# Two sliding-window and two linear-attention layers with their backward pass: from layer-by-layer stages to fused streams of token tiles

## The chip, the cores and the metric

The kernel runs on one core of a Trainium2 chip. The metric is device time in microseconds (us) of one execution; medians of a few executions are quoted. Engines are named as in the profile: PE (matrix products), PEld (its weight loads), DVE (here the multiplies and sums on whole tiles), ACT (here exp and copies), POOL (here the masks), and SP, which here issues DMA. A profile also gives the granted clock of PE as a share of full speed.

## The reference

Four residual layers on 2,048 tokens of 640 features, 32 heads of 20: linear attention (A), causal sliding-window attention of 256 tokens (B), A, B, each behind a layer norm. A and B each have one set of weights that two layers share. The outputs are the result and the gradients of the input and of the four weights.

```python
def _A_ref(x, wqkv, wo):            # q, k, v per head
    phi = lambda t: jnp.where(t > 0, t + 1, jnp.exp(t)) + 1e-6
    pq, pk = phi(q), phi(k)
    kv = einsum("bhsd,bhse->bhde", pk, v); z = einsum("bhsd->bhd", pk)
    o = (pq @ kv) / (pq . z + 1e-6)
    return o.reshape(B, S, D) @ wo
def _B_ref(x, wqkv, wo):
    scores = q @ k.T * 20 ** -0.5   # masked to 0 <= i - j < 256
    return (softmax(scores) @ v).reshape(B, S, D) @ wo
x = A_x
for f in (A, B, A, B): x = x + f(layernorm(x), ...)
# reference() returns x and jax.vjp of it for grad_out
```

Tokens go through the kernels in 16 tiles of 128. A query tile of layer B sees three key tiles: its own and the two before.

## The kernel before

It is a row of stages, each over all 16 tiles, with results in device memory between them. This is the attention part of layer B's backward pass (cuts marked with `# ...`):

```python
for g in range(G):                          # 8 groups of 4 heads
    # ... loads of QT, KT, VT, dOT, q, k, dO, O of all 16 tiles; delta on DVE
    for b in range(TT):                     # 16 query tiles
        for hh in range(4):                 # scores: 32 rows of PE each, side by side
            nc.tensor.matmul(s4[:, hh, 0:cw], lhsT=QTg[...], rhs=KTg[...], tile_position=(HPAD * hh, 0))
        for hh in range(4):
            nc.scalar.activation(p_sb[:, 0:cw], s4[:, hh, 0:cw], ACT.Exp, bias=nll[:, b, hg:hg + 1], scale=self.c_att)
            self.apply_masks(p_sb, nkt)     # two masks on POOL
        for hh in range(4):
            nc.tensor.matmul(dp_ps[:, 0:cw], lhsT=dOTg[...], rhs=VTg[...])
            nc.vector.scalar_tensor_tensor(out=ds_sb[:, 0:cw], in0=dp_ps[:, 0:cw], scalar=delta[:, b, hh:hh + 1],
                                           in1=p_sb[:, 0:cw], op0=ALU.subtract, op1=ALU.mult)
            self.transposes(dsT_ps, [ds_sb[:, i * P:(i + 1) * P] for i in range(nkt)])   # on PE
            nc.scalar.copy(dsT[:, 0:nkt, :], dsT_ps[:, 0:nkt, :])
            # ... three dQ products from dsT
        # ... dK and dV products of the key tile that is complete
self.bwd_tail(l, dqkv, ...)                 # dW of the layer, then dh and the layer norm's gradient
```

```python
def run(self):
    self.prep_weights()
    self.A_forward(0); self.B_forward(1); self.A_forward(2); self.B_forward(3)
    self.B_backward(3, first=True); self.A_backward(2, first=True)
    self.B_backward(1, first=False); self.A_backward(0, first=False)
```

The softmax here doesn't subtract the row's maximum and nothing guards it: scores larger than these inputs give would overflow.

## Time and profile before

The median was 4,575.32 us of three runs (4,571.56 to 4,575.69).

| stretch (us) | length | granted clock |
|---|---|---|
| forward, four layers (0 to 1698) | 1,698 | 0.62 to 0.81 by layer |
| dWo and dO of B3 | 88 | 0.94 |
| attention backward of B3, of B1 | 722, 721 | 0.50 |
| dW, dh and norm of B3, of B1 | 180, 192 | 0.94, 0.91 |
| backward of A2, of A0 | 435, 459 | 0.84, 0.82 |

Lines of the page of the kernel before follow: busy time of each engine, then one digit per fortieth of the span (PE's granted clock, DMA's busy share), then the DMA queues.

```profile
PE 3399.5 (74%) x31053; PEld 1892.7 (41%) x31148; DVE 2278.5 (50%) x6268; ACT 1870.0 (41%) x3758; POOL 577.0 (13%) x1963
...
PEclk6969655696865568555555996799555555798688
DMA  7345411334541136112110124214421120123312
...
q1 hardware_dynamic: 242976, 201.95, 14.5%
q10 hardware_dynamic: 263968, 205.49, 14.5%
```

No engine is at its limit on average, and DMA is far from it. The clock stands at 5 (half) in attention and near 9 in dense stages. The next lines are from the windows view of the same kernel, one row per stretch: length, busy us of each engine, clock, DMA's share, GB/s.

```profile
core 0: us, PE busy (x) PEld busy (x) DVE busy (x) ACT busy (x) POOL busy (x), PEclk, DMA share, GB/s
...
1786.00:2508.00 722.00, 607.18 (x6784) 293.58 (x6784) 344.59 (x656) 507.73 (x1282) 264.44 (x960) 0.50 0.19 47
2508.00:2688.00 180.00, 151.19 (x1035) 93.92 (x1040) 82.50 (x131) 32.08 (x65) 0.00 (x0) 0.94 0.21 70
```

Two lines of the groups view for 1786 to 2508 us: busy us and mean ns of one, then the idle time before them and who ended it.

```profile
L827 DVE SCALAR_TENSOR_TENSOR ds_sb<-dp_ps,delta,p_sb 128x384 bf16<-128x384 f32 (+2 forms) x512 | 291.1, 590 | 277.7 <-POOL p_sb L474 236.3 <-ACT dsT L834 24.1 <-PE dp_ps L823 13.2
...
L834 ACT COPY dsT<-dsT_ps 128x384 bf16<-128x384 bf16 (+2 forms) x512 | 236.3, 462 | 173.6 <-PE dsT_ps L155 155.4
```

Attention backward is a chain of exp, mask, multiply, transpose, copy and small products; DVE's multiply idles as long as it works, and waits for the mask on POOL.

### The profile page before, as it was taken

How to read it: one execution, taken by the hardware profiler on the slowest of the kernel's cores; microseconds unless marked ns; L12 is line 12 of the kernel's file. 1: busy time of each engine (PE TensorE's matmuls, PEld its weight loads, DVE VectorE, ACT ScalarE, POOL GpSimd, SP SyncE). 2: the span in 40 equal slices, each digit the busy share in tenths (PEclk: the TensorE clock that was granted, in tenths of full speed). 3: DMA queues.
4: the chain of work that ended last, by engine and by line, in shares of the span. 5: the costliest groups of instructions: out<-in, count | busy, mean ns of one | idle time of the engine just before them, and what ended most of it. 6: DMA issues, size and time to landing. Idle time of an engine off the chain costs nothing. (4 is left out here: it accounts for less than half of the span.)

```text
span 4575.2 us, 81842 instructions
## 1 busy us (share of the span) xinstructions
PE 3399.5 (74%) x31053; PEld 1892.7 (41%) x31148; DVE 2278.5 (50%) x6268; ACT 1870.0 (41%) x3758; POOL 577.0 (13%) x1963
## 2 busy tenths in 40 slices
PE   3759666675866666888888884688688888876577
PEld 2334333433433343444443453355344444354335
DVE  4764455566435542445444365444444544265436
ACT  1413445341335523777776120113677777220202
POOL 2000000000000000333333000000333333000000
PEclk6969655696865568555555996799555555798688
DMA  7345411334541136112110124214421120123312
GB/s 280 126 162 178 127 43 29 122 128 149 171 137 29 43 104 157 37 37 72 34 34 24 67 78 157 74 62 119 107 48 37 50 52 2 61 77 123 138 62 73
DMA packets 507340, 412.69 MB, mean 90 GB/s; under 512 B 329024, under 2 KB 479040, under 8 KB 505024
## 3 DMA queue, kind: packets, MB, share of 16 engines
q1 hardware_dynamic: 242976, 201.95, 14.5%
q10 hardware_dynamic: 263968, 205.49, 14.5%
q8 instruction: 245, 4.01, 0.4%
q14 instruction: 151, 1.24, 0.1%
HBM read 232.72 MB, written 174.65 MB: 89 GB/s over the span
## 5 line engine op out<-in xcount | busy, mean ns | idle before, releaser
L827 DVE SCALAR_TENSOR_TENSOR ds_sb<-dp_ps,delta,p_sb 128x384 bf16<-128x384 f32 (+2 forms) x1024 | 582.4, 590 | 555.7 <-POOL p_sb L474 472.6
L834 ACT COPY dsT<-dsT_ps 128x384 bf16<-128x384 bf16 (+2 forms) x1024 | 472.6, 462 | 346.7 <-PE dsT_ps L155 310.4
L814 ACT ACTIVATE p_sb<-s_ps,nll 128x384 bf16<-128x384 f32 (+2 forms) x1024 | 557.7, 573 | 12.4 <-issue 6.8
L155 PE MATMUL dsT_ps<-ident,ds_sb 128*128 128x128 bf16 x2880 | 499.7, 295 | 51.5 <-ACT dsT L834 40.5
L471 POOL TENSOR_SCALAR_AFFINE_SELECT p_sb<-p_sb 128x128 bf16<-128x128 bf16 x1024 | 308.6, 303 | 1583.5 <-ACT p_sb L814 1532.8
L823 PE MATMUL dp_ps<-VTg,dOTg 32*128 32x384 bf16 (+2 forms) x1024 | 439.5, 470 | 24.6 <-DVE ds_sb L827 19.5
L433 PE MATMUL sT_ps<-QTg,KTg 32*128 32x128 bf16 x2880 | 254.4, 296 | 160.4 <-DVE o_t L448 116.8
L836 PEld LDWEIGHTS <-dsT 128*128 128x128 bf16 x2880 | 156.0, 108 | 461.5 <-ACT dsT L834 393.3
L836 PE MATMUL dqvk_ps<-ksl,dsT 128*128 128x20 bf16 x2880 | 214.1, 183 | 117.8 <-ACT dsT L834 111.3
L474 POOL TENSOR_SCALAR_AFFINE_SELECT p_sb<-p_sb 128x128 bf16<-128x128 bf16 x896 | 266.9, 298 | 0.0
L807 PE MATMUL s_ps<-KTg,QTg 32*128 32x384 bf16 (+2 forms) x1024 | 240.6, 477 | 33.5 <-ACT p_sb L814 13.2
L155 PEld LDWEIGHTS <-ds_sb 128*128 128x128 bf16 x2880 | 227.4, 116 | 80.3 <-issue 68.4
L547 PEld LDWEIGHTS <-dqT 128*128 128x128 bf16 x1920 | 185.5, 99 | 132.8 <-DVE dqT L541 31.8
L543 ACT COPY dqT<-dqT_ps 128x896 bf16<-128x896 bf16 x64 | 58.0, 906 | 398.4 <-PE dqT_ps L155 391.6
L396 PE MATMUL qkvp_ps<-WBpad,hnT 128*128 128x512 bf16 x928 | 217.1, 384 | 3.6 <-ACT hnT L239 1.6
L515 PEld LDWEIGHTS <-hn_bw 128*128 128x128 bf16 x1280 | 126.9, 99 | 199.6 <-issue 74.0
L855 PEld LDWEIGHTS <-p_sb 128*128 128x128 bf16 x2880 | 156.7, 106 | 78.5 <-issue 76.2
L433 PEld LDWEIGHTS <-KTg 32*128 32x128 bf16 x2880 | 101.5, 112 | 197.2 <-DVE o_t L448 141.9
L287 PE MATMUL qkv_ps<-WA,hnT 128*128 128x512 bf16 (+1 forms) x626 | 148.5, 373 | 46.1 <-ACT vv L295 17.5
L855 PE MATMUL dqvk_ps<-dosl,p_sb 128*128 128x20 bf16 x2880 | 179.4, 181 | 3.3 <-ACT dqkv L863 2.7
L855 PE MATMUL dqvk_ps<-qsl,ds_sb 128*128 128x20 bf16 x2880 | 173.4, 179 | 0.0
L547 PE MATMUL dh_ps<-WqTB,dqT 128*128 128x320 bf16 x960 | 138.6, 304 | 25.5 <-DVE dqT L541 11.1
(2490 smaller groups left out, 5872.5 us busy)
## 6 DMA issues: line engine op xcount, KB each, us to landing
qkvp_126<-qkvp_slab SPq DMA_DIRECT2D x16, 768.0 KB, 3.5
qkvp_130<-qkvp_slab ACTq DMA_DIRECT2D x16, 768.0 KB, 3.4
qkvT_127<-qkvT_slab ACTq DMA_DIRECT2D x32, 256.0 KB, 5.2
qkvT_131<-qkvT_slab SPq DMA_DIRECT2D x32, 256.0 KB, 4.1
KTg<-qkvT_127 SPq DMA_DIRECT2D x12, 512.0 KB, 3.6
QTg<-qkvT_127 ACTq DMA_DIRECT2D x12, 512.0 KB, 4.8
QTg<-qkvT_131 ACTq DMA_DIRECT2D x12, 512.0 KB, 4.9
KTg<-qkvT_131 SPq DMA_DIRECT2D x12, 512.0 KB, 3.6
```

Of the source, the lines that this page charges most:

```text
L155: self.nc.tensor.transpose(ps[:, i, :], s, self.ident)
L433: nc.tensor.matmul(sT[:, hh, i * P:(i + 1) * P], lhsT=KTg[HPAD * hh:HPAD * (hh + 1), kt * P:(kt + 1) * P], rhs=QTg[HPAD * hh:HPAD * (hh + ...
L471: nc.gpsimd.affine_select(out=e_sb[:, last:last + P], in_=e_sb[:, last:last + P], compare_op=ALU.is_ge, fill=0.0, base=0, pattern=[[-1, P] ...
L474: nc.gpsimd.affine_select(out=e_sb[:, 0:P], in_=e_sb[:, 0:P], compare_op=ALU.is_ge, fill=0.0, base=-1, pattern=[[1, P]], channel_multiplie ...
L547: nc.tensor.matmul(ps[:, ci, 0:cw], lhsT=dqT[:, k, :], rhs=WqT[:, k, ci * cw:(ci + 1) * cw], start=(k == 0), stop=(k == QTT - 1))
L807: nc.tensor.matmul(s4[:, hh, 0:cw], lhsT=QTg[HPAD * hh:HPAD * (hh + 1), b * P:(b + 1) * P], rhs=KTg[HPAD * hh:HPAD * (hh + 1), k0 * P:(k0 ...
L814: nc.scalar.activation(p_sb[:, 0:cw], s4[:, hh, 0:cw], ACT.Exp, bias=nll[:, b, hg:hg + 1], scale=self.c_att)
L823: nc.tensor.matmul(dp_ps[:, 0:cw], lhsT=dOTg[HPAD * hh:HPAD * (hh + 1), b * P:(b + 1) * P], rhs=VTg[HPAD * hh:HPAD * (hh + 1), k0 * P:(k0 ...
L827: nc.vector.scalar_tensor_tensor(out=ds_sb[:, 0:cw], in0=dp_ps[:, 0:cw], scalar=delta[:, b, hh:hh + 1], in1=p_sb[:, 0:cw], op0=ALU.subtrac ...
L834: nc.scalar.copy(dsT[:, 0:nkt, :], dsT_ps[:, 0:nkt, :])
L836: nc.tensor.matmul(dqvk[:, hh, 2, 0:DH], lhsT=dsT[:, i, :], rhs=ksl[:, k0 + i, HPAD * hh:HPAD * hh + DH], start=(i == 0), stop=(i == nkt - 1))
L855: nc.tensor.matmul(dvk_ps[:, hh, j, 0:DH], lhsT=src_tile[:, idx * P:(idx + 1) * P], rhs=rhs_sl[:, bb, HPAD * hh:HPAD * hh + DH], start=(i ...
```

## The change

The intent is to put dense work of neighbouring tiles beside the attention chain, and to shorten the chain. Layers become streams: the output part of one layer and the first part of the next run on the same tile; layer B's attention backward runs in chunks of two query tiles, with the next chunk's dO and an earlier chunk's dh, norm and layer-A gradient as "fills". Exp, mask and multiply take two heads at once; ds is transposed by DMA; softmax's scaling is folded into other operands; weight gradients run once over both layers. All DMA stands on SP's queue. In the names below, dP is the gradient of the attention weights, ds that of the scores and dsT its transpose; a flip is a transpose on PE, a tail is a tile's dh and norm gradient, and PSUM is the memory that PE writes its products to. The diff replaces nearly the whole file (1,715 lines); its core:

```diff
-        self.B_backward(3, first=True)
-        self.A_backward(2, first=True)
-        self.B_backward(1, first=False)
-        self.A_backward(0, first=False)
+        self.forward_first()
+        self.forward_pair(0, self.x0, self.x2)
+        self.forward_pair(2, self.x2, self.out_x4)
+        self.backward_window(3, self.gs[2])
+        self.backward_linear(2, self.gs[1])
+        self.backward_window(1, self.gs[0])
+        self.weight_grads("B", (3, 1))
+        self.backward_linear(0, self.out_gx)
+        self.weight_grads("A", (2, 0))
...
+    def dma(self, out, in_, transpose=False):
+            return self.nc.sync.dma_start(out=out, in_=in_, transpose=transpose)
...
+    def core_chunk(...):     # 8 groups x 2 query tiles x 2 pairs of heads = 32 steps a chunk
+                    s = st.pS.tile([P, 2, 512], F32, name="s")          # one buffer in PSUM
+                    for j in range(2):
+                        r0 = HP * (2 * p + j)
+                        self.mm(s[:, j, 0:cw]..., Q["qT"][r0:r0 + HP, bi, gs], K["kT"][r0:r0 + HP, ...], True, True, (r0, 0))
+                    nc.scalar.activation(e[:, :, 0:cw], s[:, :, 0:cw], ACT.Exp)
+                    # ... masks on POOL, both heads at once
+                    st.q1.append(...); self.core_step(st, l); yield
+    def core_ds(...):        # st.lag1 = 2 steps later
+        dp = st.pD.tile([P, 2, 512], F32, name="dp")                     # one buffer in PSUM
+        # ... two products dp <- vT, dT
+        nc.vector.tensor_tensor(out=ds[:, :, 0:cw], in0=dp[:, :, 0:cw], in1=e[:, :, 0:cw], op=ALU.mult)
+        dT = st.pt.tile([P, 6, P], BF, name="dsT")
+        self.dma(dT, ds.rearrange("p j k -> p (j k)"), transpose=True)
+    def core_acc(...):       # st.lag2 = 3 steps later: 18 products of 20 columns for dK, dV, dQ
...
+            for c in range(NC):
+                fills = []
+                if c + 1 < NC:
+                    fills.append((before(c + 1), 18 / 32))
+                if c >= 2:
+                    fills.append((behind(c - 2), 36 / 25, 7))
+                drive(core(c), fills)
...
+    def linear_tile(self, st, l, t, WT, g_out):
+        # ... loads, flips, products into dqkv
+        self.dma(self.rows(self.dq[l], t), dqkv)
+        yield from self.tail(st, l, t, dqkv, WT, g_out)
+    def tail(...):
+        self.dma(dT, dqkv, transpose=True)
+        # ... 30 dense products dh <- dT, WT, then the norm's gradient
```

## The prediction

> **What bounds it now.** No engine does: busy shares (page) are PE 74%, DVE 50%, ACT 41%, POOL 13%. The kernel is some forty stages run one after the other, each over all 16 token tiles. From the windows view: forward 0 to 1698 us, backward 1698 to 4575. The two attention-backward stretches take 722 and 721 us, the attention-forward ones 346 each; there the granted clock is 0.50, against 0.91 to 0.97 in dense stages. In attention backward the 448 softmax-gradient multiplies keep DVE busy 267 us, but DVE idles 269 us before them, 236 of these for the POOL mask (groups view). The timeline shows the ring: exp (594 ns), two masks of about 300, multiply (616), three PE transposes, ACT copy (482), small products. Latency, not work, takes those stretches.
>
> **What the change does.** It merges stages and feeds each attention step with dense work of neighbouring tiles; exp, mask and multiply take two heads at once; ds is transposed by DMA, so 2,880 PE transposes and 1,024 ACT copies (473 us) go; per-head scalings, padded QKV and most reloads go; forward masks move from DVE to POOL; weight gradients run once over both layers. Rows drop from 62,298 to 53,554 on PE, 5,047 to 2,676 on DVE, 3,477 to 879 on ACT (instruction order). All 1,734 rows of DMA issue stand on one queue, 752 of them transposes.
>
> **Cost, estimates from traced durations.** Full-clock cadences: 320 columns 136 ns, 128 columns 56, 20 columns 27.
> - First forward: DVE 6 us a tile: 130 us.
> - Two forward pairs: PE 18 and 14 us a tile, DVE 17 and 12; the score buffer is single, so score, exp (1,450 ns), next score is a ring of some 2.2 us, eight per tile, 17.6 us. Pairs: 390 and 310 us.
> - Window backward, per chunk of two tiles: DVE 32 multiplies of 768 (1.0 us) plus 21 us, 54 us; ACT 40; PE 42 at full clock; POOL 31. With in-order stalls 60 us; eight chunks, fill and drain: 550 us each, against 993 now.
> - Linear backward 145 each; weight gradients PE 174 plus first loads, 195 each. Overlap between stages gives back 50.
>
> Sum about 2,580; I say **2,620 us** (0.57 of before), range **2,250 to 3,200**. Chances: faster by over 2% 0.97, within 2% 0.01, slower 0.02.
>
> **Transposes decide the width.** No DMA transpose is in this trace. The Trainium skill, "DMA: Bandwidth & Descriptors", section "Latency and other measured facts", gives 261 GB/s on one kernel: a 192 KB ds transpose would take 0.75 us, the 55 MB of one window layer 211 us, hidden behind 430 us of DVE. No run here shows this yet. If one ds transpose holds the queue or the engines over 1.7 us, it bounds the chunk: 3 us would mean 100 us a chunk and 3,300 in all.
>
> **Right if** the window stages are near 550 us with DVE the busiest (75% or more), clock above 0.6, ds transposes landing in 2 to 4 us, and the forward ends near 800. **Wrong if** transposes head the waits; the products waiting for dsT name it. Other ways: the clock stays at 0.50 in window stages (50 to 100 us more per layer); DVE slowed beside POOL; the one queue holding loads behind transposes that wait for ds; serial last tiles longer than I take. Better if stages overlap more, as the scheduler already hoists later weights: 2,250.
>
> By stage: forward 1,698 to about 800, weight gradients about 440 to 390, window backward without them about 1,700 to 1,100, linear backward 700 to 290.

## The result and the profile after

In rounds on one chip the kernel after took 3,537.2 us (median of four, 3,531.58 to 3,538.38) and the one before 4,573.44 (four, 4,571.24 to 4,575.69). The ratio is 0.7735, 95% interval 0.7724 to 0.7746. Ratios here are the mean time of one kernel's fast runs over that of the other's in the same rounds, so not quite the ratio of the medians quoted. Lines of the page of the kernel after:

```profile
PE 2560.2 (72%) x26776; PEld 1520.0 (43%) x26776; DVE 1562.6 (44%) x3212; ACT 1085.0 (31%) x1661; POOL 784.5 (22%) x1600
...
PEclk9888788788865565656666665566666689866699
DMA  6455444566564888787654443888886474564542
...
q1 hardware_dynamic: 964672, 527.35, 60.5%
```

PE, DVE and ACT do much less. DMA moves more (531.60 against 412.69 MB by the page), in smaller packets, and is near its limit in the two stretches of eights. The windows of the kernel after:

```profile
130.00:647.00 517.00, 402.80 (x4790) 260.08 (x4790) 285.39 (x726) 214.00 (x226) 172.96 (x292) 0.81 0.47 127
647.00:1009.00 362.00, 282.66 (x4128) 176.64 (x4128) 184.38 (x464) 175.92 (x129) 158.00 (x261) 0.81 0.60 160
1009.00:1793.00 784.00, 584.81 (x6534) 323.67 (x6534) 399.34 (x622) 274.55 (x481) 219.62 (x500) 0.60 0.75 163
1793.00:2087.00 294.00, 138.99 (x1108) 94.74 (x1109) 91.22 (x240) 45.24 (x114) 0.48 (x1) 0.69 0.47 121
2087.00:2861.00 774.00, 580.45 (x6530) 322.18 (x6529) 401.04 (x623) 274.15 (x479) 216.37 (x495) 0.60 0.70 150
...
3066.00:3347.00 281.00, 131.50 (x1102) 91.23 (x1100) 91.53 (x240) 44.64 (x112) 0.00 (x0) 0.69 0.61 164
```

| stage | predicted us | measured us |
|---|---|---|
| first forward | 130 | 130 |
| pair 0, pair 2 | 390, 310 | 517, 362 |
| window backward 3, 1 | 550, 550 | 784, 774 |
| linear backward 2, 0 | 145, 145 | 294, 281 |
| weight gradients B, A | 195, 195 | 205, 190 |
| overlap between stages | -50 | about 0 |

So 458 us of the miss lie in the window stages, 285 in the linear ones and 179 in the forward pairs.

**The linear stages** are plain to read. In the timeline of the kernel after, around one tile (start, length, in brackets the idle time before and who ended it; SPq is the issue of a DMA):

```profile
1930.15 1.73 SPq L117 DMA_TRANSPOSE dqT<-dqa  x1
...
1935.81 7.17 PE L142 MATMUL dense<-WTA,dqT 128*128 128x320 bf16 x30 [9.07 <-DMA dqT<-dqa]
...
1949.21 3.39 SPq L117 DMA_TRANSPOSE dqT<-dqa  x1
```

PE idles 9 us for the transpose of this tile's dqkv, does 30 products, and only then come the next tile's flips, products and its transpose. The tiles run one after the other, about 18 us each.

**The window stage** is not. Its steady stretch, 1150 to 1600 us, holds 171 steps of 2.63 us. Groups of that stretch in the kernel after:

```profile
L626 DVE TENSOR_TENSOR ds<-dp,e 128x768 bf16<-128x768 f32 x171 | 163.4, 955 | 103.3 <-PE dp L142 63.4 <-issue 19.4 <-POOL e L601 6.6
...
L142 PE MATMUL s<-kT,qT 32*128 32x384 bf16 x341 | 94.8, 453 | 29.1 <-ACT e L595 28.4
...
L142 PE MATMUL acc<-ks,dsT 128*128 128x20 bf16 x1026 | 72.5, 179 | 15.3 <-DMA dsT<-ds 15.0
L142 PE MATMUL dense<-WTB,dqT 128*128 128x320 bf16 x279 | 60.1, 373 | 3.4 <-DMA dqT<-dqkv 3.4
```

The multiply takes 0.96 us, as predicted, but it is busy only 36% of the stretch. PE and PEld together are occupied 381 of the 450 us and idle 69 (worked out from the trace): 28 for exp, 15 for the multiply, 15 for dsT. DMA's engines are busy 84%. No single wait explains the steady stretch. Over the whole stage, 1009 to 1793 us, dsT heads the waits of PE's products; from the waits view of the kernel after (us in total, times, longest):

```profile
PE acc L142 <- DMA dsT<-ds: 66.1, 69, 3.0
PE s L142 <- ACT e L595: 38.4, 85, 1.0
```

43.4 of the 66.1 us lie before 1150 us, in the first chunks, where no tile has a tail yet to fill with. From here on three theories were held:

- Theory 1: PE's in-order stream is the limit, at a clock that is mostly half (0.59), with score and dP pairs much dearer than costed (0.43 us a pair to the next product at half clock and 0.26 at full, where 0.16 had been costed).
- Theory 2: the transposes by DMA pace the step, by their issue (median 1.22 us each on SP in this trace), their landing or their rate.
- Theory 3, formed when runs had missed what both expected: the order in which PE's instructions stand is uneven.

### The profile page after: what moved, and what is told of

It reads as the page before. It is cut to its first block, busy times and chain, and to the rows that moved or that the text cites. A ratio compares the mean times of both kernels' runs of the same rounds, so it can differ in the third digit from the quotient of the medians.

```text
span 3536.7 us, 66383 instructions
## 1 busy us (share of the span) xinstructions
PE 2560.2 (72%) x26776; PEld 1520.0 (43%) x26776; DVE 1562.6 (44%) x3212; ACT 1085.0 (31%) x1661; POOL 784.5 (22%) x1600
## 2 busy tenths in 40 slices
DMA packets 964981, 531.60 MB, mean 150 GB/s; under 512 B 686656, under 2 KB 929344, under 8 KB 964672
## 5 line engine op out<-in xcount | busy, mean ns | idle before, releaser
L626 DVE TENSOR_TENSOR ds<-dp,e 128x768 bf16<-128x768 f32 (+2 forms) x512 | 463.5, 905 | 375.3 <-PE dp L142 269.7
L595 ACT ACTIVATE e<-s 128x768 bf16<-128x768 f32 (+2 forms) x512 | 394.7, 771 | 495.4 <-PE s L142 270.7
L597 POOL TENSOR_SCALAR_AFFINE_SELECT e<-e 128x256 bf16<-128x256 bf16 x512 | 224.9, 440 | 1224.0 <-ACT e L595 1196.3
L348 ACT ACTIVATE eT<-sT 128x1536 bf16<-128x1536 f32 (+2 forms) x256 | 351.0, 1371 | 368.8 <-PE sT L142 340.3
L142 PE MATMUL s<-kT,qT 32*128 32x384 bf16 (+2 forms) x1024 | 267.1, 436 | 91.2 <-ACT e L595 87.1
L142 PE MATMUL acc<-ks,dsT 128*128 128x20 bf16 x2880 | 216.8, 179 | 134.8 <-DMA dsT<-ds 132.9
L142 PE MATMUL acc<-qs,ds 128*128 128x20 bf16 x2880 | 277.3, 179 | 13.4 <-DVE dq L680 11.9
L142 PE MATMUL dp<-vT,dT 32*128 32x384 bf16 (+2 forms) x1024 | 254.4, 441 | 39.1 <-DVE ds L626 34.3
L142 PE MATMUL acc<-ds,e 128*128 128x20 bf16 x2880 | 269.2, 177 | 0.0
L142 PE MATMUL wg<-rq,lh 128*128 128x480 bf16 x1280 | 259.5, 366 | 0.0
L601 POOL TENSOR_SCALAR_AFFINE_SELECT e<-e 128x256 bf16<-128x256 bf16 x448 | 190.2, 425 | 0.0
```

The lines of the kernel that those rows point to most:

```text
L142: return self.nc.tensor.matmul(out, lhsT=lhsT, rhs=rhs, start=start, stop=stop, skip_group_check=True, **kw)
L348: nc.scalar.activation(e[:, :, 0:nb * P], s[:, :, 0:nb * P], ACT.Exp)
L595: nc.scalar.activation(e[:, :, 0:cw], s[:, :, 0:cw], ACT.Exp)
L597: nc.gpsimd.affine_select(out=dg, in_=dg, compare_op=ALU.is_ge, fill=0.0, base=0, pattern=[[0, 2], [-1, P]], channel_multiplier=1)
L601: nc.gpsimd.affine_select(out=fr, in_=fr, compare_op=ALU.is_ge, fill=0.0, base=-1, pattern=[[0, 2], [1, P]], channel_multiplier=-1)
L626: nc.vector.tensor_tensor(out=ds[:, :, 0:cw], in0=dp[:, :, 0:cw], in1=e[:, :, 0:cw], op=ALU.mult)
```

## The experiments

Each is an edit of the kernel after unless told otherwise. "Loops" are the two stretches from the first to the last exp of the window stages: 667 and 684 us in the kernel after.

### 1. No ds transposes

```diff
-        self.dma(dT, ds.rearrange("p j k -> p (j k)"), transpose=True)   # and the edge cases
+        dT = st.dTc          # one constant tile; the result is wrong on purpose
```

> Edit: no DMA transpose of ds; the dQ products read one constant tile, filled once (wrong dQ on purpose). Same PE, DVE, ACT, POOL work. Base: window stages 784 and 774 us, total 3537. Theory T (the DMA transposes, 1.22 us each on the issuing queue and 3.1 us to land, bound the window stages): each falls to 550-620, total 3150-3250. Theory C (PE's in-order stream at the half clock, 0.60 granted, bounds them, 85% occupied in 1150 to 1600 us): only the waits for dsT go, at most 40 us a stage; clock stays near 0.6; total 3450-3537.

Measured: 3,345.76 us (ratio to before 0.7316); loops 590 and 586. The result is wrong. In the steady stretch DMA falls from 0.84 to 0.37:

```profile
1150.00:1600.00 450.00, 402.61 (x4958) 225.56 (x4957) 295.43 (x449) 204.84 (x350) 169.65 (x387) 0.66 0.37 105
```

The transposes are worth some 95 us a stage, of a miss of about 230. Neither theory alone has this number.

### 2. Extra columns after each score and dP product

```diff
+                        self.mm(s[:, j, 384:512], self.ident, self.ident[:, 0:128], True, True)
 ...
+            self.mm(dp[:, j, 384:512], self.ident, self.ident[:, 0:128], True, True)
```

> Edit: each score and each dP product of the window stages is followed by one more product of 128 columns (identity by identity, all 128 rows) into columns 384 to 511 of its bank, which nobody reads; result stays right; 1,024 extra products a layer. Theory C, in its form that the clock falls where few columns by rows stream: granted clock in the window stages rises from 0.60 to 0.85 or more and each falls from about 780 to 600-680 although PE has more to do; total 3180-3370. Theory C without that cause of the clock: clock stays 0.6, stages grow by about 50 us each (1,024 x 107 ns less what hides). Theory T: clock may rise, stages stay within 3%.

Measured: correct, 3,980.28 us (0.8702); loops 887 and 906, clock 0.58, PE idle 7 us in the steady stretch. More work on PE does lengthen the stage; the full-height products also parted the two products of each pair, which had run side by side, so the size says little.

### 3. Linear stages: tails two tiles later

```diff
-            st = self.state(es, 2, 6)
+            st = self.state(es, 3, 6)
+            pend = []
             for t in range(TT):
-                for _ in self.linear_tile(st, l, t, wa["WT"], g_out):
+                for _ in self.linear_tile(st, l, t, wa["WT"], g_out, pend):
                     pass
+                if len(pend) > 2:
+                    for _ in pend.pop(0):
+                        pass
 ...
-        yield from self.tail(st, l, t, dqkv, WT, g_out)
+        tl = self.tail(st, l, t, dqkv, WT, g_out)
+        next(tl)             # loads and the transpose now, the rest two tiles later
+        pend.append(tl)
```

> Edit: in the two linear backward stages the tail of a tile (which needs the DMA-transposed dqkv) is emitted two tiles later, so PE has other tiles' work while the transpose flies; buffers 2 to 3. Base: 294 and 281 us, 18.4 us a tile, PE idle 9 us a tile for dqT. If the serial ring of a tile is the cause: 150-190 us each, total 3300-3360, clock of these stages from 0.69 to 0.85 or more. If the queue or the DMA engines bound them (they move 2.1 MB a tile): above 230 each, total above 3430.

Measured: correct, 3,259.7 us (0.7131), 277 us less than the kernel after. The windows of its two linear stages:

```profile
1790.00:1949.00 159.00, 118.11 (x1110) 87.06 (x1111) 92.80 (x240) 45.84 (x115) 0.81 (x2) 0.88 0.98 240
2922.00:3071.00 149.00, 116.74 (x1104) 86.61 (x1104) 93.16 (x240) 44.61 (x112) 0.00 (x0) 0.91 0.98 240
```

Shown: the linear stages' whole miss was the serial ring through the transpose. With the ring opened they take 159 and 149 us, near the predicted 145, and now fill DMA to 0.98. The prediction gives no terms for its 145, so this nearness does not show that it was costed rightly.

### 4. ds transposed on PE

```diff
-            self.dma(dT, ds.rearrange("p j k -> p (j k)"), transpose=True)
+        tp = st.ps.tile([P, 8, P], BF, name="dsT_ps", tag="m")
+        for j in range(2):
+            for i in range(nb):
+                nc.tensor.transpose(tp[:, 3 * j + i, :], ds[:, j, i * P:(i + 1) * P], self.ident)
+            nc.scalar.copy(dT, tp[:, 0:6, :])
```

> Edit: ds is transposed on PE (six 128-column transposes a step into the shared dense banks) and copied by ACT, as the kernel before did; no DMA transposes of ds; right result. Theory T: DMA share falls from 0.75 to about 0.4 and window stages fall to 650 or less each, total below 3300. Theory C with PE work at half clock: +0.36 us for 256 steps, +60 to +100 us each, total 3650-3750. Theory C with activity lifting the clock (768 more full-row columns a step): clock above 0.75 and the stages between 650 and 780; clock tells it from T, since T needs no change of clock.

Measured: correct, 3,619.33 us (0.7919), slower than the kernel after by 82; loops 702 and 727, DMA at 0.32, PE idle 20 us in the stretch. Unloading DMA at PE's cost loses: PE has no such room in this order.

### 5, 6, 7. Extra columns to lift the clock

Experiment 5 puts two extra products of 128 columns ahead of each score pair and of each dP pair, so that pairs stay together; experiment 6 puts four. Experiment 7 puts four ahead of the forward's scores.

```diff
+                    for j in range(2):       # range(4) in experiment 6
+                        self.mm(s[:, j % 2, 384:512], self.ident, self.ident[:, 0:128], True, True)
 ...
+        for j in range(2):                   # range(4) in experiment 6
+            self.mm(dp[:, j % 2, 384:512], self.ident, self.ident[:, 0:128], True, True)
```

> Edit: as e2, but the extra products (two for the score pair, two for the dP pair, 128 columns each, unread) stand before the pair, so the two 32-row products of a pair run side by side as in the changed kernel. e2 put them between and lost that (3.5 us a step, PE 98% occupied, clock 0.58). Count of columns weighted by rows: a step has 744 of its own, 512 extra, about 1,200 of dense work. Theory C with the clock set by that count: clock in the window stages 0.8 or more, loop of a stage from 667 and 684 us to 520-590, total 3280-3400. If the clock stays below 0.65: +0.43 us a step, loops 760-800, total 3700-3780, and the count is not what sets it.

> Edit: e5 with twice the extra products (eight of 128 columns a step). If the count sets the clock: 0.9 or more, but 0.43 us a step of extra PE time at full clock; loops 570-650, total 3380-3500, so slower than e5 and faster than the changed kernel. If not: clock near 0.6 and loops above 850.

> Edit: the same idea in the forward pairs alone: four unread products of 128 columns before each score group. Base: pairs 517 and 362 us at clock 0.81, PE idle 20% of 200 to 640 us. If half-clock stretches are what made PE's work there 25.8 us a tile against 18.4 costed: clock 0.95, pairs down by 20 to 60 us each in spite of 1.7 us a tile more work. If not: up by 25 to 45 us each.

Measured, all correct: experiment 5, 3,639.88 us (0.7962), loops 718 and 735, clock 0.62; experiment 6, 3,594.63 us (0.7863), loops 704 and 714, clock 0.72 to 0.74; experiment 7, 3,562.57 us (0.7803), with the clock between 200 and 640 us at up to 0.92 instead of 0.82, and no gain. The loops of experiments 5 and 6 lie between the two ranges that were expected. Twice the extra work was faster than once: activity does lift the clock. But both are slower than without, and in the forward a higher clock bought nothing. So the clock alone is not the miss.

### 8. A longer lag before dsT is used

```diff
-            st.lag1, st.lag2 = 2, 3
+            st.lag1, st.lag2 = 2, 5      # and two more buffers of e, ds, dsT
```

> Edit: the products that need dsT lag five steps instead of three behind ds (buffers of e, ds and dsT grown by two), so a transpose has two more steps to land. e1 (no transposes at all) gained 95 us a stage, of which PE's waits for dsT are 92 + 66 us by the waits view. If latency of the transposes made those waits: 40 to 80 us less per stage, total 3380-3460. If their rate (engines 84% busy) made them: less than 15 us a stage.

Measured: correct, 3,523.49 us (0.7717), 14 us less (8 by the ratios, as the kernel before was faster in these rounds too); loops 657 and 678. PE's waits for dsT halve in the stretch (15 to 7 us), and little comes of it.

### 9. Fewer dense products

```diff
             for k in range(NF):
-                self.mm(ps[:, 0:CW], dT[:, k, :], WT[:, k, c * CW:(c + 1) * CW], k == 0, k == NF - 1)
+                if k < nf:           # nf = 3 of 15 in the window stages; the result is wrong on purpose
+                    self.mm(ps[:, 0:CW], dT[:, k, :], WT[:, k, c * CW:(c + 1) * CW], k == 0, k == nf - 1)
```

> Wrong result on purpose. In the window stages alone the dense product of the tail uses 3 of its 15 contraction blocks: 24 products of 320 columns fewer per tile, 384 per stage, everything else unchanged (same transposes, loads, DVE, ACT and POOL work). Theory 1 (PE's in-order stream bounds the window stage, at a clock that is mostly half): these products take 136 ns at full and 267 ns at half clock, some 200 ns in the mix of the trace, so 77 us less PE work a stage; the two core loops of 667 and 684 us shorten by 50 to 80 us each, total 3,380 to 3,440. As less dense work may also drop the clock, the lower end is less likely. Theory 2 (transposes by DMA, their issue on one queue or their landing, pace the step): the loops move by less than 20 us each, total 3,500 to 3,540.

Measured: 3,453.42 us (0.7561), result wrong; loops 642 and 657, clock 0.54. Taking an estimated 77 us of PE work out of a stage gave 25 and 27, between what the two theories expected. The clock fell: in the first loop PE and PEld are occupied 497 us where it had been 535 (worked out from the traces), so only 38 us came off, and 25 of these show in the loop.

### 10 and 11. Four score and dP products side by side, and the control

```diff
-            st.lag1, st.lag2 = 2, 3
+            st.lag1, st.lag2 = 3, 3      # 4, 3 in the control; one or two more buffers of e
 ...
+    def follow(self, st, ins):           # called on each score, dP and small product: keeps their order
+        if st.lastp is not None:
+            self.after(ins, st.lastp)    # an order on PE, no semaphore
+        st.lastp = ins
```

With a lag of three steps the dP pair sits on the 64 rows of PE that the score pair before it leaves free; with four it sits on the same rows.

> Correct result. The dP pair is taken three steps after its scores instead of two, so that it sits on the other 64 rows of the array than the score pair issued just before it, and an order without semaphores keeps score pair, dP pair, 18 small products of each step in one row on PE (the scheduler had split a quarter of the score pairs and placed others apart). Theory 1 (PE-bound, and the pairs cost 0.43 us each at half clock and 0.26 at full because two row groups run beside each other and the array then changes over): four products side by side cost little more than two, so each step saves 0.2 to 0.4 us, 50 to 100 us a stage: total 3,340 to 3,440. Theory 2 (PE not the bound, transposes or latencies pace the step): within 20 us of 3,537, or slower by the stricter order.

> Correct result. The control of the run before: the same kept order of score pair, dP pair, small products, but the dP pair taken four steps after its scores, so that it sits on the same 64 rows as the score pair before it and cannot run beside it. Theory 1: the gain of unsplit pairs alone, 0 to 20 us a stage, total 3,490 to 3,540, slower than the run with four row groups by 60 to 200. Theory 2, that a longer distance between scores and dP or the kept order is what helps: as fast as the run with four row groups within 20 us.

Measured, both correct: 3,526.34 us (0.7721), loops 668 and 676; control 3,523.14 us (0.7714), loops 666 and 678. Where no semaphore parts them, the four do run side by side; the timeline of experiment 10 shows two pairs starting 0.01 us apart, and the next product after 0.27:

```profile
1303.51 0.34 PE L142 MATMUL s<-kT,qT 32*128 32x384 bf16 x2
1303.52 0.33 PE L142 MATMUL dp<-vT,dT 32*128 32x384 bf16 x2
1303.79 0.18 PE L142 MATMUL acc<-qs,ds 128*128 128x20 bf16 x1
```

This agrees with the Trainium skill, "TensorE: Matmul & The Clock Gate", section "The mechanism" of its part on packing small matmuls, which says that products on different row groups start about 4 ns apart and overlap. It gained nothing against the control, as theory 2 expected. But the test of theory 1 was a weak one. In the first loop 205 of 506 recorded dP products start within 60 ns of a score product (85 of 502 in the kernel after, 4 of 504 in the control), so the four ran side by side in two steps of five only. And the 27 us by which PE is occupied less came back as idle time of PE (occupied and idle 508 and 159 us, where it had been 535 and 132). PE's work was added to at a cost (2, 4, 5); taken away, it gave 25 of 38 us (9) and nothing of 27 (10).

### What the trace says then: steps are of two kinds

The trace of the kernel after was cut at each multiply on DVE, and the PE work between two multiplies counted (170 steps between 1150 and 1600 us). 87 steps have no dense product, flip or outer product: median 1.82 us, tenth percentile 1.60, with PE idle 0.5 us in the mean. 13 steps have ten dense products or more and take 4.6 to 9.8 us, 82 us together. The timeline of the kernel after shows a run of the first kind, and then one of the second (lines of PE's dP, DVE's multiply and one other on DVE):

```profile
1302.78 0.50 PE L142 MATMUL dp<-vT,dT 32*128 32x384 bf16 x2 [0.29 <-DVE ds L626]
...
1303.49 0.96 DVE L626 TENSOR_TENSOR ds<-dp,e 128x768 bf16<-128x768 f32 x1 [0.76 <-ACT e L595]
...
1304.50 0.50 PE L142 MATMUL dp<-vT,dT 32*128 32x384 bf16 x2 [0.52 <-DVE ds L626]
...
1305.20 0.96 DVE L626 TENSOR_TENSOR ds<-dp,e 128x768 bf16<-128x768 f32 x1 [0.75 <-PE dp L142]
...
1306.21 0.50 PE L142 MATMUL dp<-vT,dT 32*128 32x384 bf16 x2 [0.88 <-DVE ds L626]
...
1306.90 0.96 DVE L626 TENSOR_TENSOR ds<-dp,e 128x768 bf16<-128x768 f32 x1 [0.75 <-PE dp L142]
...
1307.92 0.50 PE L142 MATMUL dp<-vT,dT 32*128 32x384 bf16 x2 [1.13 <-DVE ds L626]
```

```profile
1309.26 0.96 DVE L626 TENSOR_TENSOR ds<-dp,e 128x768 bf16<-128x768 f32 x1 [1.00 <-issue]
1317.04 0.21 DVE L539 TENSOR_SCALAR s<-ac 128x1 f32<-128x1 f32 x1 [6.83 <-ACT dh L534]
1317.22 0.96 DVE L626 TENSOR_TENSOR ds<-dp,e 128x768 bf16<-128x768 f32 x1
```

The first fence is a ring: dP has one buffer in PSUM, so dP (0.7 us until DVE starts), multiply (0.96), next dP, 1.71 us a turn as long as dP has one buffer. The second is a lump: between two multiplies PE does 30 dense products and 47 small ones, and DVE stands for nearly 7 us. So half of the steps run at the ring's pace with PE idle for part of it, and the dense work meant to fill them comes in lumps while the ring is stopped. In the program's own order of PE's instructions the lumps are there too: the scheduler had moved the products there, away from the even places where the code emits them (a tail hands over after every five products). That the lumps cost time is a reading at this point.

### 12. No ds transposes and four side by side together

The edits of 1 and 10 together.

> Wrong result on purpose. The constant dsT (no ds transposes at all, core loops were 590 and 586 us) together with four score and dP products side by side in a kept order (alone: 668 and 676, no gain against 667 and 684). Theory 1 (PE's stream and the transposes limit together; relieved alone, the wait moves to the other): now the side-by-side products pay, 0.2 to 0.3 us a step, and the loops fall to 510 to 550 us each; total 3,210 to 3,280. Theory 2 (a third thing, such as the ring of scores and exp or the multiplies, sets the pace once the transposes are gone): the loops stay at 575 to 595 and the total at 3,330 to 3,360.

Measured: 3,380.29 us (0.7396), wrong; loops 615 and 607, slower than experiment 1 alone and outside both expected ranges. PE's work was hardly less than in experiment 1 (occupied 509 us of the first loop against 514), and only 127 of 504 dP products started beside a score product. So whether PE and the transposes hid each other's gain was not settled here.

### 13 and 14. Combined, and with a second queue

Experiment 13 has the edits of 3 and 10, with a lag of five steps before dsT is used. Experiment 14 adds:

```diff
-            return self.nc.sync.dma_start(out=out, in_=in_, transpose=transpose)
+            return (self.nc.sync if transpose else self.nc.scalar).dma_start(out=out, in_=in_, transpose=transpose)
```

> Correct result. Tails two tiles later in the linear stages (alone: 277 us less), four score and dP products side by side, and ds transposed five steps before its use instead of three (alone: 14 us less). Theory 1: with the latency of the transposes covered, PE's saving counts until the DMA engines (84 percent busy at 2.63 us a step) are full: loops 610 to 650 us each, total 3,150 to 3,230. Theory 2 (PE's saving is worth nothing in any company): loops 655 to 680, total 3,240 to 3,260.

> Correct result. The run before with every plain copy issued on the ACT queue, so that only transposes stand on SP's. If the transposes lose time because SP issues 322 of 450 us and holds copies and transposes in one row: dsT lands earlier, the loops fall by another 20 to 60 us each. If the engines' own rate or the in-order PE stream is the limit: within 15 us a loop. ACT, held by copies that wait for their data, may also make it slower.

Measured, both correct: 3,205.21 us (0.701), loops 642 and 662; with two queues 3,357.67 (0.7331), loops 678 and 678. By its total and its first loop experiment 13 lies where theory 1 had put it (3,150 to 3,230 us, 610 to 650). The three edits alone add up to 3,235 us, so together they gain some 30 us more. Plain copies on ACT's queue cost 152 us: PE idles 119 us in the stretch, and the first loop starts at 1,108 instead of 1,030 us. The Trainium skill, "DMA: Bandwidth & Descriptors", section "Issuing engines are not separate DMA queues", says that a second issuing engine saves only issue time, which is usually small. The run agrees that it does not help. The loss would fit that ACT held by issues is worse than SP held by them, but where it comes from, and how much is the wait for data at the head of ACT's queue, was not measured.

### 15, 16, 17. PE's order kept even

The even order keeps PE's instructions in the window loop as emitted (score pair, dP pair, 18 small products, then at most a few fills), and lets the tails' loads and transposes go six slots ahead, so that keeping the order does not mean waiting for them.

```diff
+    def link(self, ins):             # called on every PE instruction of the window loop
+        if self.linked:
+            if self.lastpe is not None:
+                self.after(ins, self.lastpe)
+            self.lastpe = ins
+        return ins
 ...
             def behind(c):
-                for i in range(2):
-                    t = 2 * c + i
-                    yield from self.tail(...)
-                    yield from self.a_grad(st, l - 1, t, st.gn, wa["WoT"])
+                tails = [self.tail(...) for t in ts]
+                for tl in tails:
+                    next(tl)         # loads and transposes of both tiles
+                for _ in range(6):
+                    yield
+                # ... both tails, then both a_grads
```

Experiment 15 is that alone; 16 has it with the constant dsT of 1 and a lag of three steps before dP (wrong); 17 has it with the edits of 3 and the lags of 13.

> Correct result. The changed kernel with PE's order in the loop of the window stages tied to the order of emission (score pair, dP pair, 18 small products, then at most ten dense products or one group of flips), the two tiles' tail loads issued together and six slots ahead, both tails before both linear gradients. Theory 3 (lumps of dense work stop the score and dP rings, and the steps between cannot go below the ring's 1.6 us): mean step 2.63 falls to 2.25 to 2.4, the limit then being the DMA engines' 2.2 us a step; loops 580 to 620 us each instead of 667 and 684, total 3,360 to 3,430. Theory 1 or 2 (PE's work or the transposes' latency and rate): loops 650 or more, total 3,500 or more; a stricter order could also add waits and be slower.

> Wrong result on purpose: constant dsT, no ds transposes, in the even order, dP three steps after its scores. Theory 3 with the DMA engines as the next limit: loops 470 to 540 us each, a step of 1.8 to 2.1 us (in the uneven order, without transposes, 590, and 615 and 607 with the same four products side by side); total 3,110 to 3,230. If the lumps do not matter: 580 to 615 and 3,330 to 3,390.

> Correct result. The even order with dP three steps after its scores, the transposes five steps ahead of their use, and the linear stages' tails two tiles later: what the earlier combination has (3,205 us, loops 642 and 662), with PE's order of the whole loop kept even. Theory 3: loops 570 to 610 each, total 3,070 to 3,140. Otherwise 3,190 to 3,240.

Measured: experiment 15, correct, 3,452.77 us (0.7554), loops 647 and 661; experiment 16, 3,230.01 us (0.7061), loops 556 and 552; experiment 17, correct, 3,077.62 us (0.6732), loops 597 and 617. The steady stretch of the kernel after and of 15, then of 12 and of 16, then of 13 and of 17:

```profile
1150.00:1600.00 450.00, 378.65 (x4459) 208.78 (x4459) 263.06 (x391) 185.50 (x312) 153.36 (x353) 0.59 0.84 176
...
1150.00:1600.00 450.00, 370.69 (x4731) 205.75 (x4730) 282.74 (x422) 197.86 (x332) 155.00 (x371) 0.64 0.89 183
```

```profile
1150.00:1600.00 450.00, 383.11 (x4672) 219.17 (x4670) 274.49 (x421) 195.55 (x330) 152.51 (x361) 0.63 0.35 102
...
1150.00:1600.00 450.00, 362.86 (x5148) 222.66 (x5144) 308.27 (x472) 209.44 (x364) 166.41 (x390) 0.68 0.42 121
```

```profile
1150.00:1600.00 450.00, 377.62 (x4647) 215.66 (x4647) 273.83 (x416) 197.13 (x326) 154.10 (x367) 0.62 0.89 182
...
1150.00:1600.00 450.00, 354.55 (x5226) 219.39 (x5224) 305.01 (x454) 216.42 (x369) 176.80 (x411) 0.66 0.99 197
```

Two comparisons have the even order as their main difference (with the earlier tail loads that it needs): 17 against 13 is 128 us, loops shorter by 45 each; 16 against 12 is 150 us, loops shorter by 59 and 55. Steps with ten dense products or more take 2.5 us in the mean in experiment 17, where in the kernel after it was 6.3. Alone (15) the even order gave 84 us, half of it outside the loops; the loops shortened by 20 and 23 us only, to where theories 1 and 2 had put them (650 or more), and PE waits 29 us for dsT in the stretch where it had been 15. With five steps of lag before dsT is used that wait is gone, and the total of 17 comes out as expected; the loops of 16 miss their range of 470 to 540. And in 17 DMA is at 0.99: at 2.26 us a step its engines are now full.

So it is shown that keeping PE's order, with all that comes with it, pays. That the lumps cost time through an idle PE is not shown, and the traces speak against it. The table is worked out from them for the first loop (in us; the profile models the ends of products, so take it as approximate):

| run | loop | PE or PEld occupied | both idle | dP products starting within 60 ns of a score product |
|---|---|---|---|---|
| kernel after | 667 | 535 | 132 | 85 of 502 |
| 15, even order alone | 647 | 498 | 149 | 2 of 508 |
| 12 | 615 | 509 | 107 | 127 of 504 |
| 16, the even order for 12 | 556 | 443 | 113 | 268 of 506 |
| 13 | 642 | 507 | 134 | 139 of 505 |
| 17, the even order for 13 | 597 | 436 | 161 | 300 of 506 |
| 18 | 576 | 466 | 110 | 331 of 506 |

In all three comparisons PE's occupied time fell and its idle time did not (in the second loop neither). In 16 and 17 the even order also did what experiment 10 had been meant to do: score and dP pairs run side by side in twice as many steps. The clock rose a little as well (0.60 to 0.63 in the first loop, from 13 to 17). How much of the 45 to 59 us belongs to the lumps, to the pairs, to the clock or to the earlier tail loads, no run separates. Theory 1, that PE's in-order stream limits, is thus not refuted.

### 18. Every second ds transposed on PE

On top of 17:

```diff
+        if p == 1:
+            st.tq.append((ds, dT, nb))     # two steps later: six transposes on PE, one copy on ACT
-        if nb == 3:
+        elif nb == 3:
             self.dma(dT, ds.rearrange("p j k -> p (j k)"), transpose=True)
```

> Correct result. The even combination (3,078 us; loops 597 and 617; DMA engines 99 percent busy in the steady stretch), with every second ds transposed on PE, two steps after its multiply, and copied out by ACT instead of by DMA. Theory 3 with the DMA engines as the limit that is left: DMA falls by some 0.6 us a step, PE grows by some 0.3 us a step of 1.8; step 2.0 to 2.15 us, loops 535 to 580 each, total 2,950 to 3,030. If the step is held by PE's order and its rings instead: no gain or a loss, total 3,070 to 3,180.

Measured: correct, 3,037.27 us (0.6644, interval 0.6633 to 0.6655), the fastest version; loops 576 and 600, 21 and 17 shorter. The steady stretch (1150 to 1550 us):

```profile
1150.00:1550.00 400.00, 323.60 (x4904) 219.80 (x4903) 264.41 (x398) 238.72 (x394) 151.08 (x344) 0.74 0.65 152
```

DMA falls from 0.99 to 0.65 and the clock rises to 0.74. It gains where experiment 4, the same move in the uneven order (though for all of them), lost 82 us. The gain is less than the least that was expected (48 us). In the first loop PE is occupied 30 us more than in 17 and idle 51 us less, so DMA was one limit in 17. What limits next was not tested.

## Why the prediction was right or wrong

The direction was right; the time was not: 3,537 us lie outside 2,250 to 3,200. Two steps carry most of the miss: the linear stages were costed without the ring through the transpose (shown by experiment 3), and the window chunk was costed by DVE, with PE and the ds transposes hidden behind it, where PE alone is occupied longer than the whole chunk was to take (read from the trace; its remedy is shown in part only).

- **First forward 130, weight gradients 195 each, clock in dense stages: right** (130; 205 and 190; 0.92 to 0.97).
- **"Linear backward 145 each": wrong, 294 and 281.** It was costed as throughput. The step that failed is the missing ring: a tile's dense products wait for its own transpose, and the next tile starts behind them. Experiment 3 shows it: with the ring opened the stages take 159 and 149 us, and 277 us go in all. The prediction had named "serial last tiles longer than I take", not a serial ring in every tile.
- **"Window backward, per chunk of two tiles: DVE 32 multiplies of 768 (1.0 us) plus 21 us, 54 us ... With in-order stalls 60 us ... 550 us each": wrong, 784 and 774.** In the steady stretch a chunk takes 32 x 2.63 = 84 us. DVE's work was sized right (399 us busy in the stage against 8 x 54 = 432). The step that failed is that DVE was taken as the longest engine, with PE hidden behind it and 6 us for all stalls. In the first loop PE and PEld are occupied 535 / 8 = 67 us a chunk, which alone is more than 60, and idle 132 / 8 = 16 us more; two multiplies do not follow each other at 1.0 us, since the one dP buffer makes a ring of 1.71. Keeping PE's order even takes 20 us off a loop alone and 45 to 59 in company (experiments 15, 17, 16), with less time of PE occupied and not less of it idle; which part of that change did it is open.
- **"PE 42 at full clock": mis-sized.** PE was busy 585 / 8 = 73 us a chunk of the stage, at clock 0.60. A pair was costed at 0.16 us (not said in the prediction, but its 42 comes out with it) and takes 0.26 at full and 0.43 at half clock until the next full-height product can start; dense products of 320 columns take 267 ns at half clock, 136 at full. The time hung on it in part: where PE's occupied time of the first loop fell, the loop got shorter by 25 of 38 us (9), none of 27 (10), 20 of 37 (15), 45 of 71 (17 against 13) and 59 of 66 (16 against 12).
- **"the 55 MB of one window layer 211 us, hidden behind 430 us of DVE": wrong size, and half of the sum was missing.** The Trainium skill, "DMA: Bandwidth & Descriptors", section "Latency and other measured facts", gives 261 GB/s for DMA transposes on one kernel; from that came the estimate of 0.75 us per ds transpose. In this trace the packets of 256 B (mostly the transposes') take 18 ns each when alone, 24 to 25 in the window stages, 360 and 341 us of all engines' time per stage. The other copies add some 200 to 230: 0.75 x 784 = 588 us of DMA time in a stage that was to last 550. The test that the prediction set ("wrong if transposes head the waits") does point here: over the stage dsT heads the waits of PE's products, with 66 us, though in the steady stretch it is 15 of 450. Experiment 1 (95 us a stage) and 18 (40 us in all) show its weight, and experiment 17 shows DMA as the next limit, at 0.99.
- **"ds transposes landing in 2 to 4 us": right** (median 3.1). **"Clock above 0.6": borderline**, 0.60. **"DVE the busiest (75% or more)": wrong**, 51% in the first window stage; PE was, with 75%. **"The forward ends near 800": wrong**, 1,009.
- **"Pairs: 390 and 310": wrong, 517 and 362.** PE was occupied 25.8 us a tile in the middle of pair 0 where 18 had been costed, and idle for a fifth of that stretch. Experiment 7 excludes the clock alone as the cause. No run took it further; it stays open.
- **"Overlap between stages gives back 50": wrong**, the stages abut.

Left open as well: with everything put right that was found, the loops are 576 and 600 us (18) and, without ds transposes, 556 and 552 (16), where the prediction's 60 us a chunk would make 480. PE's 436 to 466 us occupied in the loops of 17 and 18 leave little room to 480. The dP ring's 1.6 to 1.7 us in half of the steps may be part of the rest, but no run gave dP a second buffer.

## What to carry to other kernels

When dense work is to fill the gaps of a latency chain, check in the trace, step by step, that the filling sits in the gaps. When an experiment takes work off an engine, look first whether the engine's occupied time fell, and what its idle time did: experiments 10 and 12 seemed to clear PE, but in them it was occupied only 27 and 5 us a loop less than in the runs they are compared with. And when an edit pays, look for what else it changed: the even order also put pairs side by side. When transposes move from PE to DMA, sum up all DMA time of the stage with the measured time of a packet, not that of the transposes alone at a rated speed; and let nothing that needs a transpose stand in order right behind it.

## What the Trainium skill lacked or had wrong

- "DMA: Bandwidth & Descriptors": 261 GB/s for DMA transposes ("Latency and other measured facts") is too high for a mixed stage. From SBUF to SBUF the ds transposes move 256 B packets: 18 ns each when alone (an estimate of 16 x 256 B / 18 ns = 227 GB/s for 16 engines) and 24 to 25 ns beside other copies (some 165 GB/s by the same sum). The page gives no issue time measured on this chip for a transpose of 192 KB: 1.22 us median on SP here, 1.3 in the mean, against a median of 0.38 for a plain copy.
- "TensorE: Matmul & The Clock Gate", section "The mechanism": the overlap of row groups is confirmed (experiment 10), but no page gives a time for going back to full height ("TensorEngine Tiling (Array Packing)", section "Key Properties", says only that a change of tiling mode drains the array). Here the next full-height product starts 263 ns after a pair of 384 columns at full clock and 430 at half, where 384 columns at full height follow each other after 162 at full clock (the kernel before), and after an estimated 320 at half by the page's "Back-to-back issue gap".
- The same page, section "What's actually happening": two clock states and a window of some 3.4 us are confirmed (only 0.5 and 1.0 in these traces, held for multiples of 3.41 us). "Busy" is not quantified there. In these traces, columns times active rows (of 128), as a share of the window's cycles at the granted clock, tell it. In the kernel before, the windows ahead of its 40 rises had 0.68 or more, and those ahead of its falls 0.40 or less; for the 140 rises and the falls of the kernel after it is 0.73 or more and 0.41 or less. Windows at half clock without a rise behind them had 0.76 at most. A product on 32 rows counts a quarter in this sum: in the attention backward of the kernel before, all at half clock, no window has more than 0.57.
- No page has it: a scheduler may gather filling work into lumps on an in-order engine, and an order without semaphores undoes it (steps of ten dense products or more fell from 6.3 to 2.5 us in the mean here; the time gained, 150 and 128 us in two comparisons, has other parts too).
